# A transform and a gated feed-forward layer in one kernel: the loads and the written-out order of its first 20 microseconds

## The chip, the cores and the metric

The kernel runs on one core of a Trainium2 chip. A core has TensorE (PE: matrix products into PSUM), VectorE (DVE), ScalarE (ACT), GpSimd (POOL) and SyncE (SP), which here only issues transfers. The engines run side by side, each in the order of its own instruction list, and wait for one another through semaphores. PSUM has eight banks. The metric is the device time of one execution in microseconds (us): 486.74 as the median of three runs (485.81 to 487.13) before the change.

## The reference

```python
def _A_ref(x, w_r, w_i):
    X = jnp.fft.rfft2(x.astype(jnp.float32), axes=(-2, -1))
    X = X * (w_r + 1j * w_i)
    return jnp.fft.irfft2(X, s=(S, D), axes=(-2, -1)).astype(jnp.bfloat16)

def _B_ref(x, w_gate, w_up, w_down):
    return (_gelu(x @ w_gate) * (x @ w_up)) @ w_down

h  = x + _A_ref(_layernorm(x), A_w_r, A_w_i)
h2 = h + _B_ref(_layernorm(h), B_w_gate, B_w_up, B_w_down)
```

x is 2048 tokens by 576 features in bfloat16; `w_r` and `w_i` are 2048 by 289, the gate and up weights 576 by 4608, the down weight 4608 by 576. The first layer norm feeds a two-dimensional real Fourier transform, a product with a complex weight and the transform back; the second feeds a gated feed-forward layer.

## The kernel before, in words

All work is recorded by one class, `Prog`: each operation names the engine, what it reads and what it writes, and at the end the class puts in the semaphore waits that these names call for. It reorders nothing. So the order of each engine's list is the order in which the program text calls the operations, and for the first part of the kernel that order is a string, `SEQ1`, whose words are carried out one after another. A word's letter says what is done, its number for which tile, group or block, and a last letter, where there is one, on which engine (A for ScalarE, D for VectorE, P for GpSimd).

The 2048 tokens are held as 16 tiles of 128 in `XO` (tile c has the tokens 16p + c of partition p). The first part, called the front here, computes for each token the mean and the deviation, and the transform over 128 of the 2048 token positions as matrix products. The deviation is not put on the tokens but on the table of cosines and sines: `ATB` is the table as loaded (128 columns for each tile), `ATS` the same times one over the deviation (letter x, L522 on GpSimd for a whole group at once, L527 on VectorE tile by tile). The tiles form six groups: 0-1, 2-3, 4-6, 7-9, 10-12, 13-15. For each tile:

- B and b: statistics of the two halves of a tile on VectorE (L496), joined by v (L505); or, for three of the sixteen tiles, S and Q: sum and sum of squares on ScalarE (L488, L492, both read the whole tile), m on GpSimd (L499) and v (L508). Which tiles go to ScalarE is read from the string: those with a Q. They are 3, 4 and 13.
- q and c: for a group, the square root on ScalarE (L512) and the reciprocal on VectorE (L517).
- n and t: a negated copy and a copy of the last features into `XN` on GpSimd (L569, L574), read by the products.
- M: the products of a group (L553), five blocks of 2 m products each for a group of m tiles. Block n (0 to 29, five for each group) is accumulated in one PSUM bank.
- E: eviction of one block from PSUM to `U` in bfloat16 (L564) on ScalarE or VectorE. F: for blocks that have one, E evicts the first half of the columns and F the second.
- k: matmuls on zeros (L538), which nothing reads.

The bank of a block is set by its number alone, and blocks eight apart share one:

```python
def a_bank(i, k):
    return (5 * i + AORD.index(k) + ABASE) % 8
```

With `ABASE` 1 block n lies in bank (n + 1) mod 8. A block's products wait until the block eight before it has been evicted in full, halves included.

Behind the front stands the transform over the features (L642, `st_D`, tables `FT`), whose pairs of products go to two banks each, the first pair to banks 0 and 1, the next to 2 and 3; then a product with the 16-point tables `BT` (L662, `st_B`), the multiplication with the weights `WS` on VectorE (L675, `st_T`), products with the tables `VT` (L683 and L700), and the way back (L837, L854). Their evictions are at L608. `BT` and `VT` have parts for the first weight group or the tails, which are needed late (`BT1`, `VT1`). Copies of the weights to the other half of the partitions are made on GpSimd (L732) and VectorE (L730); GpSimd's may start when the last group's `ATS` is done. The rest of the kernel, from 55 us on, is the feed-forward layer (L946 and L1046), products nearly without a pause.

All loads of the front are issued by SP, through one helper at L242, in the order of the string `LORD`: a word x0-2 loads tiles 0 and 1, a word a0-4 the tables of tiles 0 to 3. Then come `FT`, the first part of `BT`, and the weight pieces.

Of the kernel before, what the change touches and what calls it, by code (L numbers as in the profile page):

```python
# [20 lines left out]
NPRE = 8  # L21
PARTS = ((0, 256), (256, 512))
GROUPS = ((0, 2), (2, 4), (4, 7), (7, 10), (10, 13), (13, 16))
SEQ1 = """B0 b0 S3 B2 Q3 n0 B1 b1 b2 n1 t0 m3P t2 v0 v1 n2 t1 q0 c0 k14 x0D q1 M0 E0A S4 m4P c1 x1D n3 E2A k104 b5 t3 b7 Q4 E1A M1 E7A B5 B6 E8A b6 B7 v2 q2 B11 E5A B8 c2 x2P E3A E9A b8 b9 B9 v3 E6A n4 B12 Q13 E4A k206 M2 b10 q3 c3 b11 S13 x3P E11A B10 t4 b12 v4 E10A B14 m13P E14A M3 q4 c4 x4P E12A E13A t5 b14 E15A b15 B15 v5 E16A E18D E17A q5 M4 E20A E19A E23A c5 x5D n5 E24A F24D F23D E21A M5 E25A E26D E22A E28D E27A E29D F25A F29D F26A F27A F28A F22A""".split()
LORD = "x0-2 x2-4 a0-4 x4-8 a4-8 x8-12 x12-16 a8-16".split()
SPLIT = tuple(int(w[1:-1]) for w in SEQ1 if w[0] == "F")
ACT_TILES = tuple(int(w[1:]) for w in SEQ1 if w[0] == "Q")
SEQF = """D2 D0 d2 D1 d0 d1 B2 D5 B0 d5 T2 D3 B1 d3 D4 T0 T1 B5 d4 D8 B3 d8 D7 T3 B4 d7 V0 D6 v0 V1 T5 d6 v1 R0 V2 r0 v2 T4 B6 D9 B8 T6 V3 d9 D11 v3 d11 B7 D10 B9 d10 V6 V4 T7 v6 v4 V5 B10 v5 R1 D12 T8 r1 d12 B11 T9 V7 D14 v7 T10 d14 D13 B12 d13 D15 T11 V9 T12 d15 v9 V8 B13 v8 R2 r2 T13 B14 T14 B15 V12 V10 v12 v10 V13 V11 T15 v13 V14 v11 v14 V15 R3 v15 r3""".split()
# [9 lines left out]
def _np_bf16(a):  # L38
    npdt = mybir.dt.np(BF16)
    return np.ascontiguousarray(np.asarray(a, dtype=np.float32).astype(npdt))  # L40
# [291 lines left out]
def _build(nc, A_x, A_w_r, A_w_i, B_w_gate, B_w_up, B_w_down, out):  # L332
    P = Prog(nc)
    T = build_tables()
    dram = {n: nc.inline_tensor(_np_bf16(T[n]), name="c_" + n.lower()) for n in T}
    PE, DVE, ACT, SP, POOL = "pe", "dve", "act", "sp", "pool"
# [52 lines left out]
    BT = sb.alloc("BT", [128, 2, 2, 128], BF16)  # L389
    VT = sb.alloc("VT", [128, 6, 2, 128], BF16)  # L390
# [12 lines left out]
    ATB = sb.alloc("ATB", [128, NT, 128], BF16)  # L403
# [32 lines left out]
    tabs = dram["ATAB"].rearrange("p (c k) -> p c k", c=NT)  # L436
# [1 line left out]
    def x_load(i, c0, c1):  # L438
        P.dma(SP, XO[:, c0:c1, 0:D], xv[:, c0:c1, :], f"x{i}", w=[("X", c) for c in range(c0, c1)])

    def atb_load(i, c0, c1):
        P.dma(SP, ATB[:, c0:c1, :], tabs[:, c0:c1, :], f"atb{i}", w=[("ATB", c) for c in range(c0, c1)])

    for i, w in enumerate(LORD):
        (x_load if w[0] == "x" else atb_load)(i, int(w[1:].split("-")[0]), int(w.split("-")[1]))
    P.dma(SP, FT[:, :, :].rearrange("p a b -> p (a b)"), dram["FTAB"][:, :], "ft", w=["FT"])
    P.dma(SP, BT[:, 0, :, :].rearrange("p b c -> p (b c)"), dram["BTAB"][:, 0:256], "bt", w=["BT"])

    def w_up(pl, hf):
        g0, g1 = ((0, 9), (9, 16))[hf]  # L450
# [5 lines left out]
    def w_down(pl, hf, sls=(0, 1, 2, 3), eng=SP, sem=""):  # L456
        g0, g1 = ((1, 9), (9, 16))[hf]
        src = (A_w_r, A_w_i)[pl].tensor
        for sl in sls:
            p0 = 64 * (sl // 2) + 32  # L460
            P.dma(eng, WS[p0 + sl % 2:p0 + 32:2, sl // 2, pl, g0:g1, :], bass.AP(src, (64 + 16 * (3 - sl) + 16 - g0) * K2, [[128 * K2, 16], [-K2, g1 - g0], [1, K2]]),
                  f"w{pl}{hf}{sem}", w=[("W", hf, pl, 2 + sl)])

    def w_zero(pl):
        for jp in range(2):
            P.dma(SP, WS[64 * jp + 32:64 * jp + 64, jp, pl, 0, :], bass.AP((A_w_r, A_w_i)[pl].tensor, (64 + 32 * jp) * K2, [[128 * K2, 16], [(-16 if jp else 48) * K2, 2], [1, K2]]),
                  f"wz{pl}", w=[("W", 2, pl, jp)])

    for pl in (1, 0):
        w_up(pl, 0)  # L470
        w_down(pl, 0)
    P.dma(SP, VT[:, 0, :, :].rearrange("p b c -> p (b c)"), dram["VTAB"][:, 0:256], "vt", w=["VT"])
    for pl in (1, 0):
        w_up(pl, 1)
        w_down(pl, 1, (0, 1, 2, 3) if pl else (0, 1))
    for pl in (1, 0):
        w_zero(pl)
    P.dma(SP, VT[:, 1, :, :].rearrange("p b c -> p (b c)"), dram["VTAB"][:, 256:512], "vt1", w=["VT1"])
    P.dma(SP, BT[:, 1, :, :].rearrange("p b c -> p (b c)"), dram["BTAB"][:, 256:512], "bt1", w=["BT1"])
    GORD = list(range(1, NG)) + [0]  # L480
    wkeys = [[("W", hf, pl, h) for pl in range(2) for h in range(6 if hf < 2 else 2)] for hf in range(3)]

# [12 lines left out]
    def ln1_half(c, h):  # L495
        P.op(DVE, lambda v: v.bn_stats(ST1[:, c, h, :], XO[:, c, 288 * h:288 * h + 288]), r=[("X", c)], w=[("ST1", c, h)])  # L496
# [59 lines left out]
    def a_ev(n, eng, late=False):  # L556
        i, k = n // 5, AORD[n % 5]
        hs = (1,) if late else (0,) if n in SPLIT else (0, 1)
        g0, g1 = 16 * hs[0], 16 * hs[-1] + 16
        c0, c1 = GROUPS[i]  # L560
        m, b, w = c1 - c0, a_bank(i, k), 128
        src = bank(b, 0, w, 0, 128 * m).rearrange("p (n g e) -> p n g e", n=m, g=32)[:, :, g0:g1, :]
        dst = U[0:w, k, g0:g1, c0:c1, :].rearrange("p g n e -> p n g e")
        fn = (lambda v: v.tensor_copy(dst, src)) if eng == DVE else (lambda a: a.activation(dst, src, ACTF.Copy))  # L564
        P.op(eng, fn, r=[("PS", b)] + ([("EV", n)] if late else []), w=[("U", i, k, h) for h in hs] + ([] if late else [("EV", n)]))
# [14 lines left out]
    ENG = {"A": ACT, "D": DVE, "P": POOL}  # L580
    RUN1 = {"k": idle_mm, "S": act_sum, "Q": act_sq, "B": lambda c: ln1_half(c, 0), "b": lambda c: ln1_half(c, 1), "v": ln1_var, "q": ln1_sqrt, "c": ln1_rs, "M": a_mm, "x": ln1_scale, "E": a_ev, "F": lambda n, eng: a_ev(n, eng, True), "n": x_neg, "t": x_tail, "m": act_mean2}
    P.op(ACT, lambda a: a.activation(SA[:, 0, 0:1], EPT[:, 0:1], ACTF.Sqrt), r=["EPT"], w=[("SA0", 0)])
    for w in SEQ1:
        a = w[1:]
        RUN1[w[0]](*((int(a[:-1]), ENG[a[-1]]) if a[-1] in ENG else (int(a),)))
# [8 lines left out]
    for t, w in enumerate(SEQF):  # L594
        k, i = w[0], w[1:].rstrip("abc")
        if k in "DBVR":
            b = min((b for b in used if b not in busy), key=lambda b: used[b])
# [4 lines left out]
        elif k in "dvr":  # L602
            b = FB[k.upper(), int(i)]
# [137 lines left out]
    c = 0  # L741
    while c < NT:
        c1 = c + 1
        while c not in ACT_TILES and c1 < NT and c1 not in ACT_TILES:
            c1 += 1
        src, f, keys = (SA[:, 0, c:c1], -1.0 / D, "SA0") if c in ACT_TILES else (MV1[:, c:c1, 0], -1.0, "MV1")
        P.op(POOL, lambda g, c=c, c1=c1, src=src, f=f: g.tensor_scalar(NM[:, c:c1], src, f, 1.0, op0=ALU.mult, op1=ALU.mult),
             r=[(keys, k) for k in range(c, c1)], w=[("NM", k) for k in range(c, c1)])
        c = c1
# [34 lines left out]
    for w in SEQF:  # L784
        i = int(w[1:].rstrip("abc"))
# [26 lines left out]
    for t, w in enumerate(SEQ):  # L812
        k, i = w[0], int(w[1:].rstrip("ADSP"))
        if k in "INu":
            b = min((b for b in range(2 * ing, 4) if b not in held), key=lambda b: last[b])
# [3 lines left out]
        elif k in "ioUEae":  # L819
            b = SLOT[{"i": "I", "o": "N", "U": "u", "E": "I", "a": "N", "e": "u"}[k], i] // 2  # L820
# [145 lines left out]
    for w in SEQ:  # L966
        a = w[1:]
# [53 lines left out]
    for j, c in enumerate(range(NPRE, NT)):  # L1021
        f = DEF0 + DSTEP * j
# [77 lines left out]
def bass_sequential_preLN__spectral_gfnet__geglu_ffn__prompt_kernel(  # L1100
    nc, A_x, A_w_r, A_w_i, B_x, B_w_gate, B_w_up, B_w_down, out
):
    _build(nc, A_x, A_w_r, A_w_i, B_w_gate, B_w_up, B_w_down, out)
# [28 lines left out]
```

## Time and profile before

| what | value |
|---|---|
| median of three runs | 486.74 us (485.81 to 487.13) |
| the profiled execution | 485.97 us |
| its span | 484.2 us |
| PE busy | 477.5 us (99%) |
| DVE, ACT, POOL busy | 183.3, 146.3, 52.2 us |
| first product of L553 | 7.08 us |
| first product of L642 | 19.91 us |

The profile records one execution. Its page gives for each engine the busy time and the share of the span; a chain view follows the work that ended last back from the end; a timeline lists the instructions of an engine in order of time, merged where they are alike, with the idle time ahead of an instruction and what released it in brackets. A line such as L553 is that line of the kernel before; in the kernel after, the lines from 486 to 582 have numbers smaller by two. DMA-issuing instructions stand under SPq or POOLq; the time from issue to landing is listed with them.

### The profile page before, as it was taken

The numbers are of one execution on the slowest core, as the hardware profiler recorded it, in microseconds if no ns is written. First come the engines' busy times: TensorE is split into PE (matmuls) and PEld (weight loads), VectorE is DVE, ScalarE is ACT, GpSimd is POOL, SyncE is SP. The second block draws the span as 40 slices with busy tenths as digits, with TensorE's granted clock in tenths as the row PEclk, the third lists the DMA queues.
The fourth block names the chain that finished last, engine by engine and source line by source line (L and its number), as shares of the span: only waits on it lengthen the run. The fifth ranks groups of instructions, "written<-read, shape, count | busy, mean of one in ns | idle before, by whom it ended". The sixth has DMA issues, their size and how long they took to land.

```text
span 484.2 us, 12895 instructions
## 1 busy us (share of the span) xinstructions
PE 477.5 (99%) x5875; PEld 304.4 (63%) x5876; DVE 183.3 (38%) x366; ACT 146.3 (30%) x295; POOL 52.2 (11%) x88
## 2 busy tenths in 40 slices
PE   8999999999999999999999999999999999999998
PEld 4877765555588744444688644444788544445884
DVE  7898755665500144333200234333101233333011
ACT  6998753434300032233100132223100133223000
POOL 6873317010120000000000000000000000000000
DMA  8865889941430001000000011000000000000000
GB/s 283 215 142 160 251 279 282 374 109 27 173 100 27 26 15 23 20 1 0 3 14 15 26 24 23 13 1 1 3 14 27 14 1 1 0 1 1 3 26 26
DMA packets 28582, 33.19 MB, mean 69 GB/s; under 512 B 12640, under 2 KB 21872, under 8 KB 28528
## 3 DMA queue, kind: packets, MB, share of 16 engines
q1 hardware_dynamic: 24864, 19.87, 14.3%
q0 software_dynamic: 3664, 12.50, 8.1%
q8 instruction: 46, 0.75, 0.7%
q14 instruction: 8, 0.07, 0.1%
HBM read 26.21 MB, written 2.36 MB: 59 GB/s over the span
## 4 chain that ended last, share of the span: by engine, by line
PE 95%; DMA 1%; DVE 1%; POOL 1%; SPq 0%; issue 0%; POOLq 0%; DVEq 0%
PE PS L946 58%; PE PS L1046 27%; PE PS L642 2%; PE PS L1058 2%; PE PS L683 2%; DMA XO<-in_A_x_dram 1%; PE PS L553 1%; PE PS L662 1%; PE PS L837 1%; PE PS L996 1%; DVE XO L860 1%; SPq L242 0%; PE PS L1013 0%; PE PS L854 0%; POOL XN L569 0%
## 5 line engine op out<-in xcount | busy, mean ns | idle before, releaser
L946 PE MATMUL PS<-HT,WG 64*128 64x512 bf16 (+1 forms) x2142 | 233.5, 373 | 0.1
L946 PEld LDWEIGHTS PS<-HT,WG 64*128 64x128 bf16 x2142 | 116.1, 94 | 104.4 <-DVE AT L955 0.2
L954 ACT ACTIVATE GL<-PS 128x512 bf16<-128x512 f32 x144 | 85.7, 596 | 281.7 <-PE PS L946 281.7
L955 DVE TENSOR_TENSOR AT<-GL,PS 128x512 bf16<-128x512 bf16 x144 | 98.8, 687 | 166.0 <-ACT GL L954 166.0
L1046 PE MATMUL PS<-WD,AT 64*128 64x288 bf16 x2160 | 133.0, 283 | 0.0
L1046 PEld LDWEIGHTS PS<-WD,AT 64*128 64x128 bf16 x2160 | 114.3, 94 | 18.7
L1033 DVE TENSOR_TENSOR OS<-PS,XO 128x288 bf16<-128x288 f32 (+2 forms) x32 | 13.2, 452 | 125.5 <-PE PS L1046 118.0
L946 PE MATMUL PS<-HT,WGX 64*128 64x512 bf16 x486 | 53.5, 376 | 0.0
L946 PEld LDWEIGHTS PS<-HT,WGX 64*128 64x128 bf16 x486 | 25.7, 94 | 26.7
L863 ACT ACTIVATE OS<-XO,NM 128x576 bf16<-128x576 bf16 x15 | 11.6, 773 | 11.4 <-DVE XO L1017 11.4
L642 PE MATMUL PS<-FT,U 64*128 64x288 bf16 x160 | 13.3, 283 | 0.0
L675 DVE TENSOR_TENSOR TP<-YS,WS 128x1024 bf16<-128x1024 bf16 x16 | 11.0, 686 | 0.4 <-PE PS L683 0.2
L564 ACT ACTIVATE U<-PS 128x384 bf16<-128x384 f32 (+2 forms) x31 | 10.5, 427 | 1.2 <-PE PS L553 1.1
L496 DVE BATCH_NORM_STATS2 ST<-XO 128x6 f32<-128x288 bf16 x26 | 10.0, 441 | 1.8 <-DMA XO<-in_A_x_dram 1.8
L242 POOL DMA_DIRECT2D WG<-in_B_w_gate_dram x9 | 6.1, 679 | 35.5 <-DMA WG<-in_B_w_gate_dram 32.1
L683 PE MATMUL PS<-VT,TP 64*128 64x128 bf16 x256 | 9.9, 217 | 0.0
L553 PE MATMUL PS<-ATS,XO 128*128 128x128 bf16 x96 | 8.2, 220 | 1.5 <-POOL ATS L522 0.8
L242 POOL DMA_DIRECT2D WD<-in_B_w_down_dram x9 | 6.7, 756 | 22.9 <-PE PS L1013 22.9
L608 ACT ACTIVATE CUS<-PS 128x576 bf16<-128x576 f32 x14 | 9.1, 656 | 0.4 <-PE PS L642 0.2
L1058 PE MATMUL PS<-WD,AT 128*128 128x448 bf16 (+1 forms) x72 | 9.0, 286 | 0.0
L538 PE MATMUL PS<-ZD 128*128 128x512 bf16 x23 | 7.5, 484 | 1.5 <-POOL ZD L431 1.5
L608 ACT ACTIVATE YS<-PS 128x576 bf16<-128x576 f32 x14 | 8.8, 653 | 0.1
(88 smaller groups left out, 231.3 us busy)
## 6 DMA issues: line engine op xcount, KB each, us to landing
WD<-in_B_w_down_dram POOLq DMA_DIRECT2D x9, 576.0 KB, 13.0
WG<-in_B_w_up_dram SPq DMA_DIRECT2D x6, 576.0 KB, 6.6
WG<-in_B_w_gate_dram POOLq DMA_DIRECT2D x6, 576.0 KB, 6.2
out_dram<-OS SPq DMA_DIRECT2D x30, 72.0 KB, 1.7
XO<-in_A_x_dram SPq DMA_DIRECT2D x3, 576.0 KB, 7.1
WGX<-in_B_w_up_dram SPq DMA_DIRECT2D x2, 576.0 KB, 4.5
WGX<-in_B_w_gate_dram POOLq DMA_DIRECT2D x2, 576.0 KB, 5.8
HT<-HN SPq DMA_TRANSPOSE x60, 2.4
```

The costliest lines, as they stand in the source:

```text
L242: fn = lambda e: e.dma_start(out_ap, in_ap)
L553: P.op(PE, lambda t, b=b, lhs=lhs, p0=p0, p1=p1, s=s, e=e, o=o, c=c: t.matmul(bank(b, p0, p1, o, o + 128), lhs, ATS[:, c, :], start=s, sto ...
L608: fn = (lambda v: v.tensor_copy(dst, src)) if eng == DVE else (lambda a: a.activation(dst, src, ACTF.Copy))
L642: return P.op(PE, lambda t: t.matmul(bank(b0 + o, 0, 128, 0, 2 * HK), U[64 * h:64 * h + 64, us, 2 * i:2 * i + 2, :, :], FT[64 * h:64 * h + ...
L683: return P.op(PE, lambda t: t.matmul(bank(b0 + o, 0, 128, 128 * c, 128 * c + 128), TP[64 * h:64 * h + 64, z, o, t_, c:256:2], VT[64 * h:64 ...
L863: P.op(ACT, lambda a, c=c, out=out: a.activation(out, XO[:, c, 0:D], ACTF.Square, bias=NM[:, c:c + 1], accum_out=SB2[:, 1, c:c + 1]), r=[( ...
L946: op = P.op(PE, lambda t, h0=h0, kt=kt, wt=wt, b=b, s=(not second and j == 0), e=(second and j == n - 1): t.matmul(bank(b, 0, 128, c0, c1) ...
L954: P.op(ACT, lambda a: a.activation(GL[:, s2, :], bank(b0), ACTF.Gelu_apprx_tanh), r=[("PS", b0)], w=[("GL", s2)])
L955: P.op(DVE, lambda v: v.tensor_tensor(AT[:, f, :], GL[:, s2, :], bank(b0 + 1), op=ALU.mult), r=[("GL", s2), ("PS", b0 + 1)], w=[("AT", f)])
L1033: P.op(DVE, lambda v: v.tensor_tensor(OS[:, p % 2, d0:d1], bank(b, 0, 128, 0, d1 - d0), XO[:, c, d0:d1], op=ALU.add), r=[("PS", b), ("X", ...
L1046: e[h] = P.op(PE, lambda t, f=f, h=h, r0=r0, j=j: t.matmul(bank(b0 + h, 0, 128, 0, 288), AT[r0:r0 + 64, f, 128 * p:128 * p + 128], WD[r0:r ...
L1058: P.op(PE, lambda t, b=b, d0=d0, d1=d1, f=f, j=j: t.matmul(bank(b, 0, 128, 0, d1 - d0), AT[:, f, 128 * p:128 * p + 128], WD[:, f, d0:d1], ...
```

## The change

Four things are changed together.

- `LORD`: the tiles are loaded in two-tile pieces (0-1, 2-3, 4-5, 6-7, 8-9, 10-11) and one piece of four (12-15) one after another; the tables of tiles 8 to 15 follow as before.
- The tables of tiles 0 to 3 and 4 to 7 are issued by ScalarE, behind its dummy square root; the second waits until tiles 0 and 1 have landed.
- `BT` is loaded whole in one transfer, and `VT`'s first two parts in one, at the places of the first transfers of each; the two later transfers are gone from SP's list.
- `SEQ1` is a new order of the front. The tiles on ScalarE are 3, 5 and 9. The scale of groups 0 and 1 is on GpSimd (x0P, x1P) in place of VectorE. The idle matmuls k104 and k206 are gone, k14 stays. The blocks evicted in halves are 25, 27, 28 and 29, all halves on ScalarE; VectorE evicts blocks 18, 23 and 24 whole.

```diff
-SEQ1 = """B0 b0 S3 B2 Q3 n0 B1 b1 b2 n1 t0 m3P t2 v0 v1 n2 t1 q0 c0 k14 x0D q1 M0 E0A S4 m4P c1 x1D n3 E2A k104 b5 t3 b7 Q4 E1A M1 E7A B5 B6 E8A b6 B7 v2 q2 B11 E5A B8 c2 x2P E3A E9A b8 b9 B9 v3 E6A n4 B12 Q13 E4A k206 M2 b10 q3 c3 b11 S13 x3P E11A B10 t4 b12 v4 E10A B14 m13P E14A M3 q4 c4 x4P E12A E13A t5 b14 E15A b15 B15 v5 E16A E18D E17A q5 M4 E20A E19A E23A c5 x5D n5 E24A F24D F23D E21A M5 E25A E26D E22A E28D E27A E29D F25A F29D F26A F27A F28A F22A""".split()
-LORD = "x0-2 x2-4 a0-4 x4-8 a4-8 x8-12 x12-16 a8-16".split()
+SEQ1 = """b1 t0 B1 b0 S3 n0 n1 B0 m3P t1 B2 v0 Q3 b2 v1 q0 q1 c0 S5 Q5 x0P k14 M0 b4 c1 B4 E1A B7 x1P m5P t2 B6 b6 v2 n2 b8 S9 b7 m9P q2 c2 B10 B8 Q9 v3 E0A b11 x2P E3A E4A M1 E2A q3 b10 E5A B11 E6A c3 M2 E9A t3 E11A b12 B12 E7A n3 v4 E8A q4 E13A x3P n4 b15 B14 E10A M3 c4 E14A B15 E12A b14 E15A B13 x4P E16A b13 v5 t4 q5 n5 E19A E18D M4 c5 E17A x5D E21A t5 E20A E23D E22A M5 E26A E27A E24D E25A E28A E29A F27A F28A F25A F29A""".split()
+LORD = "x0-2 x2-4 x4-6 x6-8 x8-10 x10-12 x12-16 a8-16".split()
-    def atb_load(i, c0, c1):
-        P.dma(SP, ATB[:, c0:c1, :], tabs[:, c0:c1, :], f"atb{i}", w=[("ATB", c) for c in range(c0, c1)])
+    def atb_load(i, c0, c1, eng=SP, r=()):
+        P.dma(eng, ATB[:, c0:c1, :], tabs[:, c0:c1, :], f"atb{i}", r=r, w=[("ATB", c) for c in range(c0, c1)])
-    P.dma(SP, BT[:, 0, :, :].rearrange("p b c -> p (b c)"), dram["BTAB"][:, 0:256], "bt", w=["BT"])
+    P.dma(SP, BT[:, :, :, :].rearrange("p a b c -> p (a b c)"), dram["BTAB"][:, :], "bt", w=["BT", "BT1"])
-    P.dma(SP, VT[:, 0, :, :].rearrange("p b c -> p (b c)"), dram["VTAB"][:, 0:256], "vt", w=["VT"])
+    P.dma(SP, VT[:, 0:2, :, :].rearrange("p a b c -> p (a b c)"), dram["VTAB"][:, 0:512], "vt", w=["VT", "VT1"])
-    P.dma(SP, VT[:, 1, :, :].rearrange("p b c -> p (b c)"), dram["VTAB"][:, 256:512], "vt1", w=["VT1"])
-    P.dma(SP, BT[:, 1, :, :].rearrange("p b c -> p (b c)"), dram["BTAB"][:, 256:512], "bt1", w=["BT1"])
     P.op(ACT, lambda a: a.activation(SA[:, 0, 0:1], EPT[:, 0:1], ACTF.Sqrt), r=["EPT"], w=[("SA0", 0)])
+    atb_load(8, 0, 4, ACT)
+    atb_load(9, 4, 8, ACT, [("X", 0)])
```

## The prediction

> **What bounds the kernel now.** I read the page first: TensorE (PE) is busy almost throughout, and the chain that ended last is PE work too. So a change to the front shows in the total as the time by which the first stage behind it, the products of L642, starts earlier or later; behind that PE runs on in its order, and nothing of it is edited.
>
> ```profile
> PE 477.5 (99%) x5875; PEld 304.4 (63%) x5876; DVE 183.3 (38%) x366; ACT 146.3 (30%) x295; POOL 52.2 (11%) x88
> PE 95%; DMA 1%; DVE 1%; POOL 1%; SPq 0%; issue 0%; POOLq 0%; DVEq 0%
> ```
>
> Next the chain over the first 75 us. It waits for the token tiles 8 to 11 until 10.14, then for GpSimd, and from 14.53 on it is PE alone: two stretches of L553, then L642.
>
> ```profile
> 3.06 7.08 DMA XO<-in_A_x_dram
> 11.65 0.83 POOL ATS L522
> 13.64 0.84 POOL ATS L522
> 14.53 1.85 PE PS L553 x30
> 16.47 3.51 PE PS L553 x60
> 19.98 2.01 PE PS L642 x30
> ```
>
> Then the timelines of three queues: SP's issues (start, length), PE, and ScalarE (ACT). From 11.78 to 20.84 ACT has no idle note: it is as full as PE in the front, and it empties the PSUM banks that PE fills.
>
> ```profile
> 1.64 0.43 SPq L242 DMA_DIRECT2D ATB<-c_atab  x1
> 2.11 0.43 SPq L242 DMA_DIRECT2D XO<-in_A_x_dram  x1
> 3.06 0.91 SPq L242 DMA_DIRECT2D XO<-in_A_x_dram  x2
> ...
> 10.46 1.24 PE L538 MATMUL PS<-ZD 128*128 128x512 bf16 x5
> 12.54 0.23 PE L553 MATMUL PS<-ATS,XO 128*128 128x128 bf16 x1 [0.84 <-POOL ATS L522]
> 19.91 2.08 PE L642 MATMUL PS<-FT,U 64*128 64x288 bf16 x30
> ...
> 7.85 0.68 ACT L488 ACTIVATE JNK<-XO 128x576 bf16<-128x576 bf16 x1
> 8.51 0.37 ACT L564 ACTIVATE U<-PS 128x256 bf16<-128x256 f32 x1
> 15.00 2.00 ACT L564 ACTIVATE U<-PS 128x384 bf16<-128x384 f32 x5
> 16.85 0.34 ACT L512 ACTIVATE RS<-MV,EPT 128x3 f32<-128x3 f32 x1
> 17.03 3.81 ACT L564 ACTIVATE U<-PS 128x384 bf16<-128x384 f32 x13
> 21.05 1.26 ACT L608 ACTIVATE CUS<-PS 128x576 bf16<-128x576 f32 x2 [0.20 <-PE PS L642]
> ```
>
> Last the transfers' issues with their time to landing, taken stretch by stretch (size, us to landing):
>
> ```profile
> ATB<-c_atab SPq DMA_DIRECT2D x1, 128.0 KB, 4.0
> XO<-in_A_x_dram SPq DMA_DIRECT2D x1, 576.0 KB, 5.5
> ATB<-c_atab SPq DMA_DIRECT2D x1, 128.0 KB, 5.8
> XO<-in_A_x_dram SPq DMA_DIRECT2D x1, 576.0 KB, 7.1
> ATB<-c_atab SPq DMA_DIRECT2D x1, 256.0 KB, 8.4
> ```
>
> Issue plus time gives the landings: tiles 0-1 at 3.6, 2-3 at 4.5, tables 0-3 at 5.6, tiles 4-7 at 7.6, tables 4-7 at 8.4, tiles 8-11 at 10.1, 12-15 at 11.5, tables 8-15 at 12.4.
>
> **The change, part by part.** *Loads.* SP still issues eight transfers before the one for FT, so each later slot stays (0.43 us each). In place of two table loads among the tiles there are four two-tile pieces, and both small table loads go to ACT. The time that matters, called t8, is the landing of tiles 8-9. Counted in KB landed, 1440 of tiles and 256 of tables stand ahead of its end: 1696, half way between 1408 (8.4) and 1984 (10.1), so 9.26. Bounds: 6.95, if each of three pieces takes the 0.82 us that lay between tiles 0-1 and 2-3 and the tables cost nothing; 10.1, if each takes the 1.2 us of the slowest step (tables 0-3) and the tables keep their 1.2 and 0.8. I take 9.26, since the bytes are the same and only their order is new.
> The Trainium skill ("DMA: Bandwidth & Descriptors", section "Issuing engines are not separate DMA queues") says that transfers started by different engines run on the same 16 DMA engines and interleave, so that a second issuer saves only issue time. By it the tables still stand ahead, and 9.26 holds; without it the table bytes drop out, 1440 KB are left, and t8 is 8.5, a sum 0.8 us lower. No row of before has a load on ACT's queue.
>
> *ACT's issues.* Two of about 0.43 us (SP's row), at 2.2 behind the table load and the dummy square root, and at 3.7 behind tiles 0-1. ACT idled 2.18 us there until 4.40, so they cost nothing; if tiles 2-3 landed before 4.15, they would cost the difference. The first table load is issued 0.6 later than now; 4.0 us on it lands at 6.2. GpSimd then has just ended L574 for tiles 2-3 (0.30+0.62+0.62+0.26+0.30 with gaps of 0.1, from 3.75), and the first scale, moved from VectorE's two of 0.21 to one on GpSimd of about 0.6 (0.83 for 384 columns), starts at 6.6 behind the reciprocal. So the first L553 starts at 7.3, not 7.08. That 0.2 is covered by what follows.
>
> *ACT's queue.* The new list puts the sum and square of tile 9 (S9, Q9) behind one eviction of the first group (E1A) and ahead of all its others. E1A is issued at about 7.95 and ACT is free at 8.2; then S9 stands and waits for tiles 8-9, with E0A, E3A, E4A and E2A queued behind it. Block n goes to bank (n+1) mod 8, so block 8 (the fourth of M1) waits for E0A and M2's first block (10) for E2A. Steps from the rows: S or Q 0.66 (7.85 to 8.51), square root 0.18 between evictions, an eviction of 256 columns 0.275, of 384 0.37 (five in 1.85), of 192 0.255. E0A starts at t8 + 0.66 + 0.18 + 0.66 + 0.06 = t8+1.56 and E2A ends at t8+2.77: 12.0. M2 began at 12.54 before, so here 0.5 is won. GpSimd's scale of that group is done at 11.5 (S9's sum, 0.3, 0.9) and lies beside the wait.
>
> *The end of ACT's queue.* From S9 on ACT holds: S9 and Q9 1.32, four square roots 0.72, nine evictions of 256 columns 2.46, thirteen of 384 4.81, and six halves up to F25A with its own end 1.90: 11.2, with 0.1 for two short waits 11.3. F25A frees bank 2, and the second L642 set (D0) writes banks 2 and 3. So D0 starts at t8 + 11.3 = 20.56. Before it started at 20.16 (19.91 plus four of L642 at 0.061, ten taking 0.61). The loss is 0.4 us; break-even is t8 = 8.86, and from there each microsecond of t8 costs one. PE itself would be ready sooner: M3 at 13.8, M4 15.7, M5 17.4 to 19.1, against 19.8; what it wins is lost in front of D0, because the four second halves, of which VectorE had some before, are all on ACT now.
>
> *Fillers.* Ten idle matmuls (L538, 1.03 and 1.24 us) go. They stood in waits, so nothing is won. PE is then idle from 9.1 to 11.2 in M1, where the longest idle before, once PE ran fast, was 0.84. I take its cost at nothing; the other end is the first rival.
>
> *Tables of the 16-point stage.* BT and VT as one transfer each: 64 KB more in front of the w loads (about 0.2 us at 288 KB in 0.82), two issues (0.58, 0.43) gone from SP at 25 to 26. BT was needed first at 21.8 and landed at 14.4, VT at 26.6 and landed at 20.1; the w copies on VectorE start at 20.8 and have slack until 22.9. SP's next wait is at 29.2. Nothing; were the w loads 1 us late, up to the whole of it.
>
> Sum: +0.4. The profiled execution took 485.97 (span 484.2 and 1.8 around it), so 486.4; the runs' median lies 0.77 above it, so 487.1, with 0.1 for the extra bytes 487.2.
>
> **The rivals.**
> *PE goes slow in the gap (slower).* At the start L538 needs 0.427 us a matmul for 4.2 us, then 0.216: there is a slow state, and the fillers may have held it off. If the idle 2.1 us bring it back, some 39 of M2's and M3's products take 0.11 (twice the warm 0.056, as 0.427 is of 0.216) instead: 2.0 us, M5 ends at 21.1, F25A at about 21.8, D0 1.6 to 1.8 later than before: 488.5. It decides once the slow stretch passes 1.5 us, PE's slack ahead of D0. For it: the fillers are gone where the gap is longest. Against: 0.84 idle in 12.54's neighbourhood left the products at 0.056.
> The Trainium skill ("TensorE: Matmul & The Clock Gate", section "Why this matters for your kernels") advises against PE-idle gaps over about 3 us between bursts, since a whole idle window brings the half rate back. By that rule 2.1 us would not, and the sum stays; a gap grown by 1 us would. No row of before tests it.
> *The table loads on ACT land late (slower).* S9 cannot start before the landing of tables 0-3 + 1.7 (scale, the first block, E1A). At 6.2 that is hidden; at 2.25 + 5.8 (row of tables 4-7) = 8.05 it replaces t8 by 9.75: 487.6; beyond 8.6 it is over 488.2. The 8.4 row is the far end.
> *The pieces land early.* At t8 of 8.2 or less E1A bounds S9: D0 at 19.5, 0.6 won, 486.1. For it: from 9 to 12 us the windows show 405 to 418 GB/s, at which three pieces take 2.1 us. It is a floor, since the rest of ACT's queue is unchanged.
> *The change does more behind the front* (SP freer from 25 us): nothing waits there; 485.2 or less, if at all.
>
> **How the numbers follow.** Forecast 0.44 (487.2, own range 486.4 to 488.3 with t8 from 8.5 to 10.1), slow PE 0.24, late tables 0.14, early pieces 0.13, gain behind 0.05. 0.3% is 1.46 us, about what a measurement of this kernel can tell from no change (three runs lie within 1.3). Slower by that: 0.24x0.8 + 0.14x0.6 + 0.44x0.12 = 0.33. Faster: 0.05 and a tenth of the early case, 0.06. Same: 0.61. The range runs from the early case, less 0.2 of spread, to slow PE with 0.3: 485.9 to 488.8.
>
> **What would show it.** Right: ACT idle before L488 of tile 9 on a tile transfer until about 9.3; PE idle about 2 us in the second L553 set with an ACT eviction as releaser; L642 with a gap of near 1 us after its first products; products at 0.056 throughout. Wrong: products at 0.11 after 11; the first scale waiting for ATB; ACT idle at the end of the front; S9 starting at 8.2.

## The result and the profile after

The kernel after takes 487.62 us (median of ten executions, 487.21 to 488.95), the kernel before 486.46 beside it (ten, 485.81 to 487.35). The ratio is 1.0029, with a 95% interval of 1.0020 to 1.0038: a small loss, real, and about as large as a measurement of this kernel can tell. The forecast was 487.2 in a range of 485.9 to 488.8; it started from 486.74, the median of three, so the change that was forecast is +0.46, and the one measured is +1.16. The profiled execution of after took 487.71 us (span 485.9), that of before 485.97 (span 484.2), so the two traces lie 1.7 us apart where the medians lie 1.16 apart; the one of before happens to be a quick one.

The page of after, busy time by engine and then the shares of the chain that ended last, is still TensorE's:

```profile
PE 476.3 (98%) x5866; PEld 279.5 (58%) x5866; DVE 183.8 (38%) x358; ACT 146.3 (30%) x295; POOL 54.1 (11%) x91
PE 93%; DVE 2%; ACT 2%; DMA 1%; POOL 1%; issue 0%; SPq 0%; DVEq 0%
```

PE is busy 1.2 us less than before and the kernel is longer all the same, so PE waits more. TensorE's timeline in after shows where (start, length, operation; in brackets the idle time ahead and its releaser):

```profile
8.06 0.23 PE L551 MATMUL PS<-ATS,XO 128*128 128x128 bf16 x1 [1.09 <-POOL ATS L520]
...
10.94 0.40 PE L551 MATMUL PS<-ATS,XO 128*128 128x128 bf16 x4 [0.93 <-ACT U L562]
12.19 0.22 PE L551 MATMUL PS<-ATS,XO 128*128 128x128 bf16 x1 [0.63 <-ACT U L562]
...
14.55 0.22 PE L551 MATMUL PS<-ATS,XO 128*128 128x128 bf16 x1 [0.52 <-POOL ATS L520]
...
20.09 0.47 PE L642 MATMUL PS<-FT,U 64*128 64x288 bf16 x4
21.16 1.77 PE L642 MATMUL PS<-FT,U 64*128 64x288 bf16 x26 [0.60 <-ACT U L562]
```

The first product comes at 8.06 (before 7.08). By 14.55, the fourth group, both kernels are level (before 14.53). The first set of L642 starts at 20.09 (before 19.91), but only four of its thirty products run; the other 26 stand until 21.16, where they ran at 20.16 before. So 1.0 us is lost in front of the second set, 0.60 of it as PE's idle time with an eviction of ScalarE as its releaser.

ScalarE's timeline in after, its DMA issues (ACTq) included:

```profile
0.73 1.28 ACT L580 ACT_TABLE_LOAD   x1 [0.73 <-PEq L1117]
0.86 0.33 ACTq L242 DMA_DIRECT2D ATB<-c_atab  x1
2.03 0.20 ACT L580 ACTIVATE SA<-EPT 128x1 f32<-128x1 f32 x1
4.43 0.33 ACTq L242 DMA_DIRECT2D ATB<-c_atab  x1
5.35 0.68 ACT L486 ACTIVATE JNK<-XO 128x576 bf16<-128x576 bf16 x1 [3.12 <-DMA XO<-in_A_x_dram]
...
9.01 0.67 ACT L486 ACTIVATE JNK<-XO 128x576 bf16<-128x576 bf16 x1
...
13.06 1.04 ACT L562 ACTIVATE U<-PS 128x384 bf16<-128x384 f32 x3 [0.35 <-PE PS L551]
...
19.06 2.27 ACT L562 ACTIVATE U<-PS 128x384 bf16<-128x384 f32 x9 [0.41 <-PE PS L551]
```

Three things are to be seen. The first table load was issued at 0.86, while the engine was still loading its activation table: it stands behind the dummy square root in the program, but nothing makes it wait for it. The sum of tile 9 at 9.01 has no idle note, so tiles 8-9 were there already. And the last nine evictions run in one row from 19.06; the eighth of them, the second half of block 25, ends at 21.1 and frees the bank for which PE stands.

The transfers in after (size, us from issue to landing) at 0.73 and 0.86, at 2.59 (tiles 8-9), and at 4.43:

```profile
XO<-in_A_x_dram SPq DMA_DIRECT2D x1, 288.0 KB, 3.7
ATB<-c_atab ACTq DMA_DIRECT2D x1, 128.0 KB, 3.7
...
XO<-in_A_x_dram SPq DMA_DIRECT2D x1, 288.0 KB, 5.4
...
ATB<-c_atab ACTq DMA_DIRECT2D x1, 128.0 KB, 6.2
```

Issue plus time, each transfer by itself, gives the landings:

| what | before | after |
|---|---|---|
| tiles 0-1 | 3.7 | 4.4 |
| tiles 2-3 | 4.4 | 5.3 |
| tables 0-3 | 5.7 | 4.6 |
| tiles 4-5, 6-7 | 7.7 | 6.5, 7.2 |
| tiles 8-9, 10-11 | 10.1 | 8.0, 8.7 |
| tables 4-7 | 8.4 | 10.6 |
| tiles 12-15 | 11.5 | 10.5 |
| tables 8-15, the last of 2816 KB | 12.4 | 11.1 |

So the first four tiles come 0.7 to 0.9 us later and all later tiles 0.4 to 2.2 us earlier; tables 4-7 come 2.2 later. (The 3.6 and 4.5 of the prediction for the first two pieces are 3.7 and 4.4 when each issue is read by itself, so the step between them is 0.7 and not 0.82. Only its lower bound for tiles 8-9 rests on that.)

Behind the front, the first product of L837 starts at 44.77 against 43.62 (+1.15), and then the products wait longer for `VR`. TensorE's timeline in after, and below it the same place before:

```profile
44.77 1.16 PE L837 MATMUL PS<-DT,V 64*128 64x288 bf16 x16 [0.38 <-DVE V L608]
46.70 0.35 PE L837 MATMUL PS<-DT,VR 64*128 64x288 bf16 x2 [0.77 <-DMA VR<-RB]
...
57.20 1.05 PE L946 MATMUL PS<-HT,WG 64*128 64x256 bf16 x16
```

```profile
43.62 1.16 PE L837 MATMUL PS<-DT,V 64*128 64x288 bf16 x16 [0.38 <-DVE V L608]
45.10 0.34 PE L837 MATMUL PS<-DT,VR 64*128 64x288 bf16 x2 [0.33 <-issue]
```

From the first product of L837 to the first with `VR` it is 1.93 us after and 1.48 before, so 0.45 more. The first product of L946 starts at 57.20 (before 55.47): 1.7 us, all of the difference of the two traces.

### The profile page after: what moved, and what is told of

It is laid out like the page before. It is cut to its first block, busy times and chain, and to the rows that moved or that the text cites. A ratio compares the mean times of both kernels' runs of the same rounds, so it can differ in the third digit from the quotient of the medians.

```text
span 485.9 us, 12874 instructions
## 1 busy us (share of the span) xinstructions
PE 476.3 (98%) x5866; PEld 279.5 (58%) x5866; DVE 183.8 (38%) x358; ACT 146.3 (30%) x295; POOL 54.1 (11%) x91
## 4 chain that ended last, share of the span: by engine, by line
PE 93%; DVE 2%; ACT 2%; DMA 1%; POOL 1%; issue 0%; SPq 0%; DVEq 0%
PE PS L946 58%; PE PS L1046 27%; PE PS L1058 2%; PE PS L642 1%; DVE ST L494 1%; PE PS L551 1%; DMA XO<-in_A_x_dram 1%; PE PS L683 1%; DMA VR<-RB 1%; PE PS L996 1%; DVE XO L860 1%; PE PS L662 1%; ACT YS L608 1%; ACT CUS L608 0%; PE PS L837 0%
## 5 line engine op out<-in xcount | busy, mean ns | idle before, releaser
L946 PE MATMUL PS<-HT,WG 64*128 64x512 bf16 (+1 forms) x2142 | 233.3, 372 | 0.1
L946 PEld LDWEIGHTS PS<-HT,WG 64*128 64x128 bf16 x2142 | 105.9, 94 | 114.4 <-DVE AT L955 0.2
L1046 PEld LDWEIGHTS PS<-WD,AT 64*128 64x128 bf16 x2160 | 103.3, 94 | 29.8
L946 PE MATMUL PS<-HT,WGX 64*128 64x512 bf16 x486 | 53.4, 376 | 0.0
L946 PEld LDWEIGHTS PS<-HT,WGX 64*128 64x128 bf16 x486 | 23.2, 94 | 29.2
L863 ACT ACTIVATE OS<-XO,NM 128x576 bf16<-128x576 bf16 x15 | 11.6, 774 | 11.4 <-DVE XO L1017 11.4
L642 PE MATMUL PS<-FT,U 64*128 64x288 bf16 x160 | 13.5, 283 | 0.7 <-ACT U L562 0.6
L494 DVE BATCH_NORM_STATS2 ST<-XO 128x6 f32<-128x288 bf16 x26 | 10.1, 440 | 2.5 <-DMA XO<-in_A_x_dram 2.5
L562 ACT ACTIVATE U<-PS 128x384 bf16<-128x384 f32 (+2 forms) x31 | 10.3, 437 | 0.8 <-PE PS L551 0.8
L551 PEld LDWEIGHTS PS<-ATS,XO 128*128 128x128 bf16 x96 | 6.8, 98 | 4.4 <-ACT U L562 2.1
```

The costliest lines, as they stand in the source:

```text
L551: P.op(PE, lambda t, b=b, lhs=lhs, p0=p0, p1=p1, s=s, e=e, o=o, c=c: t.matmul(bank(b, p0, p1, o, o + 128), lhs, ATS[:, c, :], start=s, sto ...
L642: return P.op(PE, lambda t: t.matmul(bank(b0 + o, 0, 128, 0, 2 * HK), U[64 * h:64 * h + 64, us, 2 * i:2 * i + 2, :, :], FT[64 * h:64 * h + ...
L946: op = P.op(PE, lambda t, h0=h0, kt=kt, wt=wt, b=b, s=(not second and j == 0), e=(second and j == n - 1): t.matmul(bank(b, 0, 128, c0, c1) ...
L1046: e[h] = P.op(PE, lambda t, f=f, h=h, r0=r0, j=j: t.matmul(bank(b0 + h, 0, 128, 0, 288), AT[r0:r0 + 64, f, 128 * p:128 * p + 128], WD[r0:r ...
```

## The experiments

Two causes were to be told apart. **T, the tail:** the last evictions, with all second halves on ScalarE, hold the bank of the second set of L642. **L, the loads:** the table load that ScalarE issues at 0.86 runs beside the first tiles and delays everything that starts from them. Each kernel is the changed one with one edit, unless its diff says otherwise; the lines of L642 and L837 have numbers lower by one or two where load lines are taken out. The times of before beside them are 486.38 (35 executions) for four of the kernels (the tail alone, the first table in SP's list, the old loads, the old order) and 486.56 (29) for the other four. Each ratio and its interval come from the executions and are not exactly the quotient of the two medians.

**The tail alone.** The words behind block 23 are put in such an order that VectorE evicts block 24 ahead of M5, and behind M5 block 26, the first half of 28 and both halves of 29; on ScalarE the second half of 25 comes ahead of those of 27 and 28.

```diff
-... E20A E23D E22A M5 E26A E27A E24D E25A E28A E29A F27A F28A F25A F29A
+... E20A E23D E24D E22A M5 E25A E26D E27A E28D F25A E29D F27A F28A F29D
```

> The changed kernel with another order of the last evictions alone: blocks 26, 28 and both halves of 29 on VectorE, F25A in front of F27A and F28A on ScalarE; loads as changed. Theory T (tail): nine evictions in a row on ScalarE behind the second block of M5 (19.06 to 21.1) hold bank 2, and the second set of L642 starts at 21.16; with four of them on VectorE it starts at about 20.4, the first set stays at 20.1, and the time falls by 0.7, to 486.9. Theory L (loads): the loss comes from tiles 0 to 3 landing 0.8 us late; then the tail matters by 0.2 at most, 487.4.

Measured 486.43 us, ratio to before 0.9999 (0.9983 to 1.0015). The timelines of this kernel, ScalarE's, VectorE's and TensorE's:

```profile
19.32 1.06 ACT L562 ACTIVATE U<-PS 128x192 bf16<-128x192 f32 x4 [0.34 <-PE PS L551]
...
18.04 2.69 DVE L562 CAST U<-PS 128x384 bf16<-128x384 f32 x6
...
7.97 0.23 PE L551 MATMUL PS<-ATS,XO 128*128 128x128 bf16 x1 [1.84 <-POOL ATS L520]
...
19.88 2.07 PE L642 MATMUL PS<-FT,U 64*128 64x288 bf16 x30
```

Four evictions stand in ScalarE's last row where nine did, and VectorE does six from 18.04 on. The thirty products of L642 run in one piece from 19.88; four at 0.061 into it, the second set starts at 20.12, 1.04 earlier than in the changed kernel. That is 0.3 more than the 20.4 expected. The first product of the front is as late as there (7.97). T is shown, and the loss is gone with this edit alone. Which part of it does so, the sharing or the earlier second half of block 25, is not told apart.

**The first table in SP's list.** Tables 0 to 3 return to SP's third place, the second table load stays on ScalarE.

```diff
-LORD = "x0-2 x2-4 x4-6 x6-8 ...
+LORD = "x0-2 x2-4 a0-4 x4-6 x6-8 ...
-    atb_load(8, 0, 4, ACT)
```

> The changed kernel with the tables of tiles 0 to 3 back in SP's third slot; those of tiles 4 to 7 stay on ScalarE. Theory L: tiles 0-1 land at 3.7 again and not at 4.4, statistics, GpSimd's queue and the first L551 move 0.7 forward, L642 starts at about 19.4, its second set at 20.4, and the time falls by 0.7, to 486.9. Theory T: what is won at the start is lost in front of the tail, the second set of L642 stays near 21, 487.4. If the landing of tiles 0-1 stays at 4.4, it was not the table load on ScalarE that delayed it.

Measured 486.75 us, ratio 1.0004 (0.9988 to 1.0020). Its timelines, VectorE's first statistics and TensorE's L642 (here L641):

```profile
3.74 1.90 DVE L494 BATCH_NORM_STATS2 ST<-XO 128x6 f32<-128x288 bf16 x5 [1.82 <-DMA XO<-in_A_x_dram]
...
20.58 1.76 PE L641 MATMUL PS<-FT,U 64*128 64x288 bf16 x26 [0.60 <-ACT U L562]
```

The statistics start at 3.74 where after has 4.43, and the second set comes 0.58 earlier; the idle 0.60 with ScalarE as its releaser is untouched. So L is shown as well, as a cause of its own: the delay of 0.7 at the first tile is 0.6 at the end of the front, and T stands behind it unchanged. It is the trace that shows it; the interval of the time reaches up to 1.0020, where that of the changed kernel begins.

**Both edits together.**

> The changed kernel with both repairs: the tables of tiles 0 to 3 in SP's third slot, and the last evictions shared with VectorE. Theory: the two losses lie one behind the other (0.6 at the first tiles, 1.1 at the second set of L642), so both gains add: L642 starts at about 19.3 without a gap, 0.6 earlier than before, 485.8 against 486.4. Rival: VectorE or GpSimd bound the front by then, and the second gain is lost: 486.4.

Measured 486.09 us, ratio 0.9990 (0.9981 to 1.0000). TensorE's timeline:

```profile
19.32 2.07 PE L641 MATMUL PS<-FT,U 64*128 64x288 bf16 x30
...
43.67 1.16 PE L836 MATMUL PS<-DT,V 64*128 64x288 bf16 x16 [0.34 <-DVE V L607]
```

The second set is at 19.32 + 0.24 = 19.56: 1.60 earlier than in the changed kernel, against 1.04 + 0.58 from the two edits alone. In the front they add up. The front now ends 0.6 earlier than before the change, but L837 starts at 43.67, where it started at 43.62: in this profile the gain has gone on the way through the stages between. The time is the lowest of all that were run, 0.5 below before where 0.6 was expected, and its interval reaches to no change.

**All loads in SP's list.** As the last, and the second table load too returns to SP, behind tiles 6-7.

```diff
-LORD = "x0-2 x2-4 a0-4 x4-6 x6-8 x8-10 ...
+LORD = "x0-2 x2-4 a0-4 x4-6 x6-8 a4-8 x8-10 ...
-    atb_load(9, 4, 8, ACT, [("X", 0)])
```

> The kernel with both repairs, and the tables of tiles 4 to 7 in SP's list too, behind tiles 6-7: nothing is issued by ScalarE. They land at about 8.3 in place of 10.5; tiles 8-9 land 0.4 to 0.8 later, at 8.4 to 8.8, where the sum of tile 9 starts at 8.4 anyhow. GpSimd's scale of the third group stands behind that sum. If the issue by ScalarE buys nothing: the same as with both repairs, within 0.3. If it buys 0.4 or more: slower by as much.

Measured 486.47 us, ratio 1.0000 (0.9986 to 1.0015). The transfers issued at 3.07, and TensorE's timeline:

```profile
ATB<-c_atab SPq DMA_DIRECT2D x1, 128.0 KB, 4.8
```

```profile
19.25 2.07 PE L640 MATMUL PS<-FT,U 64*128 64x288 bf16 x30
...
45.88 0.35 PE L835 MATMUL PS<-DT,VR 64*128 64x288 bf16 x2 [1.57 <-DMA VR<-RB]
```

Tables 4 to 7 land at 7.9 instead of 10.3 in the last kernel, and that moves L642 by 0.07: nothing was waiting for them there. All 2816 KB have landed at 4.97 + 6.5 = 11.4, against 12.4 before, on the same single queue: the smaller pieces alone account for most of the earlier landings. The front is as short as in the last kernel and L837 starts at 43.16, but the wait for `VR` is 1.57 in this profile, which eats that.

**The old loads under the new order.** `LORD` as before the change, nothing issued by ScalarE, the new `SEQ1`.

```diff
-LORD = "x0-2 x2-4 x4-6 x6-8 x8-10 x10-12 x12-16 a8-16".split()
+LORD = "x0-2 x2-4 a0-4 x4-8 a4-8 x8-12 x12-16 a8-16".split()
-    atb_load(8, 0, 4, ACT)
-    atb_load(9, 4, 8, ACT, [("X", 0)])
```

> The new order (and the joined 16-point tables) with the loads of before. The prediction's formula: tile 9 lands with tiles 8 to 11 at 10.14, ScalarE waits for it until then, the second set of L642 starts at 10.14 + 11.3 = 21.4, 1.3 later than before: 487.8. Theory L alone: tiles 0-1 at 3.7 give back 0.7, so 486.9. Theory T: the tail costs 0.8 in any case, 487.3 or more.

Measured 488.40 us, ratio 1.0033 (1.0017 to 1.0050). ScalarE's and TensorE's timelines:

```profile
8.00 0.68 ACT L486 ACTIVATE JNK<-XO 128x576 bf16<-128x576 bf16 x1 [1.16 <-DMA XO<-in_A_x_dram]
...
10.46 0.68 ACT L486 ACTIVATE JNK<-XO 128x576 bf16<-128x576 bf16 x1 [0.76 <-DMA XO<-in_A_x_dram]
...
14.76 1.04 ACT L562 ACTIVATE U<-PS 128x384 bf16<-128x384 f32 x3 [0.58 <-PE PS L551]
...
12.41 0.61 PE L551 MATMUL PS<-ATS,XO 128*128 128x128 bf16 x4 [2.29 <-ACT U L562]
...
22.34 1.77 PE L640 MATMUL PS<-FT,U 64*128 64x288 bf16 x26 [0.60 <-ACT U L562]
```

Here ScalarE does stand in front of the sums of tile 5 (1.16) and tile 9 (0.76), as the prediction had it for tile 9 in the changed kernel, and the second set comes 1.2 later still, 0.9 later than the 21.4 expected. Of that 0.9, 0.3 is the tile's (10.46 for 10.14). The other 0.6 is ScalarE's wait ahead of 14.76 for products that ran at half rate: here the prediction's first rival came. PE had stood idle for 2.29, and its products from 12.41 to 15.15 follow each other 0.107 apart and not 0.056 (four of them take 0.61 in the row above, 0.40 at the same place in after); the granted clock is 0.50 in these three microseconds.

So the new order needs the smaller pieces: with them it takes its sums without a wait and PE's idle time stays short; with the old ones it loses on both.

**The new loads under the old order.** `SEQ1` as before the change, the rest as after.

> The changed loads with the order of before. Theory L: first statistics at 4.4, the first L553 at about 7.9 (7.08 before), VectorE reaches the third group 0.5 late and stays late: 486.9, between the two kernels. Theory T or a fault of the new order in general: 486.4, as before, or less, since tiles 8 to 11 land 1.5 to 2 us earlier than before.

Measured 487.15 us, ratio 1.0021 (1.0004 to 1.0037). TensorE's timeline:

```profile
8.44 0.23 PE L551 MATMUL PS<-ATS,XO 128*128 128x128 bf16 x1 [2.37 <-DVE ATS L525]
...
21.10 2.08 PE L642 MATMUL PS<-FT,U 64*128 64x288 bf16 x30
```

The old order has no gap in L642, but all of it is 1.2 late, from the first product on (8.44, before 7.08). The profiled execution took 488.18, 1.0 above the median of the eleven, so this 1.2 is not to be set against the 0.8 of the medians. The late first tiles cost this order its whole front, and the earlier later tiles bring it nothing: GpSimd waits 0.79, 0.40 and 0.24 for VectorE's reciprocals, so it is VectorE, which starts on the first tile, that is late.

**The 16-point tables alone.** The kernel before with `BT` and `VT` in one transfer each and nothing else changed.

> The kernel before with the joined 16-point tables alone. Prediction and both theories: nothing, 486.4; the last products with VR (L837) wait 0.3 as before. If the joined tables are what makes those products wait longer in the changed kernel (0.77), the wait grows here too and the time rises by 0.4.

Measured 486.73 us, ratio 1.0001 (0.9991 to 1.0010): no effect on the time. TensorE's timeline:

```profile
20.12 2.08 PE L640 MATMUL PS<-FT,U 64*128 64x288 bf16 x30
...
46.01 0.34 PE L835 MATMUL PS<-DT,VR 64*128 64x288 bf16 x2 [0.69 <-DMA VR<-RB]
```

This profile has the order of before and reaches L642 0.2 later, and the products with `VR` 0.9 later. That is what one profile may differ by from another behind the front; readings there of less than a microsecond prove little.

**Both table loads held back.** In the changed kernel the first table load on ScalarE waits for tiles 0-1 and the second for tiles 2-3.

```diff
-    atb_load(8, 0, 4, ACT)
-    atb_load(9, 4, 8, ACT, [("X", 0)])
+    atb_load(8, 0, 4, ACT, [("X", 0)])
+    atb_load(9, 4, 8, ACT, [("X", 2)])
```

> The changed kernel with both table loads on ScalarE held until tiles have landed: the first until tile 0, the second until tile 2. If the early issue alone delays tiles 0 and 1, they land at 3.7. If a load on ScalarE's queue is served slowly behind SP's long list (6.0 to 6.8 us for the second table so far, against 3.7 for the first into an empty queue), the first tables land at about 9.8, the first L551 starts at 10.5 and the time rises to 489 or more. If the queue alone costs nothing, they land at 7.5, the first L551 starts at 8.2, as changed, and the time stays at 487.6.

Measured 490.71 us (two executions), ratio 1.0086 (1.0062 to 1.0110). GpSimd's timeline, and below it the transfers issued between 3.6 and 3.8:

```profile
10.34 1.37 POOL L520 TENSOR_TENSOR ATS<-ATB,RS 128x256 bf16<-128x256 bf16 x2 [4.00 <-DMA ATB<-c_atab]
```

```profile
XO<-in_A_x_dram SPq DMA_DIRECT2D x1, 576.0 KB, 6.5
ATB<-c_atab ACTq DMA_DIRECT2D x1, 128.0 KB, 6.6
```

Issued at 3.68, the 128 KB are there at 10.3, and GpSimd stands four microseconds for them. The first product comes at 11.01, 2.95 later than in the changed kernel, the second set of L642 3.0 later, and the time is 3.1 above the changed kernel's. PE had stood idle for 3.68 by then, and its first 26 products came 0.107 apart here too; that hardly shows at the second set, since GpSimd's list, 3.0 late, sets the pace behind it. At that moment SP's seven tile loads are all issued, and the small load on the other queue lands together with the 576 KB that SP issued beside it: a second queue gives no right of way. In SP's third place (tables 0 to 3, 1.65), with the small pieces behind it, the same 128 KB took 3.0 to 3.1. So the early issue at 0.86, which costs 0.7 to 0.9 at the first tiles, is still far better than a later one on this queue; the cheap place is in SP's list. This bears out the rule of the Trainium skill ("DMA: Bandwidth & Descriptors", section "Issuing engines are not separate DMA queues") by which transfers of all issuers share the engines and a second issuer saves issue time only.

## Why the prediction was right, and where it was wrong

The direction, the place (the second set of L642, held by an eviction of ScalarE) and the size class were right. The size was low: +0.4 at the second set and +0.5 in all were forecast, +1.0 and +1.16 came. Inside, two of its steps failed, in opposite directions, and a third thing, how full GpSimd's list is, was not seen. Of the four signs that it named, two came (the gap in L642 and products at 0.056 throughout); ScalarE's wait for tile 9 did not, and the two microseconds of idle PE came in pieces.

- **Loads: wrong.** t8 was to be 9.26, "since the bytes are the same and only their order is new". It was 8.0. Smaller pieces land sooner for the same bytes: 1280 KB were there at 7.2 (before 7.7), 2816 KB at 11.1 (12.4), and at 11.4 in one queue. And only one table stood ahead of tiles 8-9, since the one issued at 4.43 landed at 10.6. The estimate without the table bytes, 8.5, was too late as well.
- **ScalarE's issues: wrong.** They were put at 2.2 and 3.7, at no cost. The first went out at 0.86, inside the engine's table load, which ran until 2.01: an issue with nothing to wait for did not stand behind it. It landed at 4.6 and not 6.2, so the first scale never waited for it; but tiles 0-3 landed 0.7 to 0.9 late, and the first product came at 8.06 instead of 7.3. That the price is 0.6 to 0.7 in the front was shown by putting the load back.
- **ScalarE's queue: the number right, the reason wrong.** The sum of tile 9 was to start at 9.26 behind a wait for the tile. It started at 9.01 with no wait, as the rival of early pieces had it; that rival's 486.1 failed because the eviction ahead of the sum came at 8.74, not 7.95, on account of the late first tiles, and because 12.15 and not 11.3 followed the sum. Two errors of 1.3 and 0.8 thus nearly cancelled: that the sum's start came out 0.25 from the forecast is luck. M2's first block started at 12.19 for a forecast of 12.0, and that is luck too (next point). The wait itself is real where the tiles come late: 0.76 with the old loads.
- **The end of ScalarE's queue: right in kind, too small.** From the sum of tile 9 to the second set 11.3 was counted, with 0.1 in it for waits; it took 21.16 - 9.01 = 12.15. Of the missing 0.85, 0.66 is the two waits for PE, 0.35 and 0.41, less the 0.1 that was counted. Behind both stands GpSimd, and this is the term that was not counted: with two more scales on it GpSimd's list is full.

  The first wait, ahead of 13.06, is for M2's second block. M2 began at 12.19. The row names ScalarE as the releaser, but the eviction that M2's first block needs had ended at 11.7, and the scale of M2's tiles ends on GpSimd at 11.22 + 0.83 = 12.05. In all six kernels with the new order and the small pieces M2 begins 0.14 to 0.15 after that scale, whatever ScalarE does. The kernel with all loads in SP's list shows it: ScalarE's row ends at 11.38, the scale at 11.33, and PE starts at 11.48, 0.15 behind the scale and only 0.10 behind the eviction, where in after these are 0.14 and 0.5.

```profile
10.20 1.18 ACT L562 ACTIVATE U<-PS 128x256 bf16<-128x256 f32 x4
...
10.50 0.83 POOL L520 TENSOR_TENSOR ATS<-ATB,RS 128x384 bf16<-128x384 bf16 x1 [0.17 <-POOL TM L497]
...
11.48 0.22 PE L551 MATMUL PS<-ATS,XO 128*128 128x128 bf16 x1 [0.24 <-ACT U L562]
```

  The prediction had that scale done at 11.5, beside the wait. The second wait, ahead of 19.06, is for M5, whose products were to be ready at 17.4 and ran at 18.19, right behind M4. M3 and M4 ran at 14.55 and 16.51 for 13.8 and 15.7, again 0.14 to 0.15 after the ends of GpSimd's scales (14.40 and 16.37). GpSimd's timeline in after:

```profile
7.39 1.37 POOL L520 TENSOR_TENSOR ATS<-ATB,RS 128x256 bf16<-128x256 bf16 x2 [0.31 <-DVE RS L515]
...
11.22 0.83 POOL L520 TENSOR_TENSOR ATS<-ATB,RS 128x384 bf16<-128x384 bf16 x1 [0.17 <-POOL TM L497]
...
13.57 0.83 POOL L520 TENSOR_TENSOR ATS<-ATB,RS 128x384 bf16<-128x384 bf16 x1 [0.17 <-DVE MV L503]
14.56 0.83 POOL L567 TENSOR_SCALAR XN<-XO 128x768 bf16<-128x768 bf16 x1 [0.16 <-POOL ATS L520]
15.54 0.83 POOL L520 TENSOR_TENSOR ATS<-ATB,RS 128x384 bf16<-128x384 bf16 x1
```

From 7.39 to 18.15 it has no idle stretch over 0.2. (The 0.17 ahead of 13.57 is GpSimd's usual gap, though the row names VectorE: the reciprocal that the scale needs had been ready since 12.53.) The scale of the fourth group starts at 13.57, as before (13.64), although two of its three tiles, 8 and 9, landed 2.2 earlier. With the first table back in SP's list GpSimd's first scale starts at 6.69 and M3 at 13.96: the list moves with its start, by 0.70 and 0.59, less a longer wait there for tables 4-7. So PE could not be sooner than before at M3 while the first tiles were late, and the tail's delay stood on top. This is read from the timelines; no run takes a scale off GpSimd.

- **"What it wins is lost in front of D0, because the four second halves ... are all on ACT now": right** in place and engine: with the last evictions reordered and shared the gap is gone and so is the loss. That it is the halves alone is not shown.
- **Fillers: right in this kernel, in part by luck.** PE stood for 0.93 and 0.63 with eight products between (some 2 in one piece were forecast), and for 1.09 ahead of the first product, and all products that follow start 0.056 apart. The rival of a slow PE (488.5) did not come, but only because the idle time came in pieces: with the old loads PE stood for 2.29 in one piece, about what was forecast here, and 26 products followed 0.107 apart, as that rival had it (there it cost 0.6 at the second set, where the rival's 1.6 to 1.8 lie 1.2 to 1.4 above the forecast's 0.4). Idle time of 3.68 (both loads held back) did the same, and 2.37 ahead of the first product of the old order did not. What decides between 2.29 and 2.37 is not shown. The rule of the Trainium skill ("TensorE: Matmul & The Clock Gate", section "Why this matters for your kernels"), by which PE should have no idle gaps over some 3 us, would have let the 2.29 pass; the measurement differs, and it decides.
- **`BT` and `VT`: right**, shown alone (1.0001).
- **Late tables (487.6): did not come** in the changed kernel; the kernel with the loads held back shows the mechanism at its far end.
- **Behind the front: 0.45 that no step had**, the longer wait for `VR`. The last transfer of `VR` is issued by GpSimd, as in before, in a group of five that starts 3.5 us ahead of L837, as before; it landed 5.07 us after the first of the five (41.28 to 46.35; it is issued at 43.22 and takes 3.1), before after 4.4 (40.07 to 44.4; issued at 42.02, it took 2.4). The idle time at that place was 0.77 here and 0.43, 0.72, 0.69, 0.40, 1.57 and 0.78 in six of the experiments, in none of them in step with the edit; in the other two no such wait was in the way. The joined tables alone do not bring it, since those other two have them as well. What sets it is open. The median's 1.16 leaves room for little more than the 1.0 of the front, so part of the 0.45 may belong to that one profile.

## What to carry to other kernels

A load moved to another engine's queue goes out when that engine's sequencer reaches it, not when the engine is free (0.86 here, in a table load that ran until 2.01), and it competes with what others issued (tiles 0-1 took 3.7 and not 2.9): where it should land is decided by what is issued ahead of it, so keep a small urgent load in its place in one list. When evictions are dealt out at the end of a stage, count for each PSUM bank that the next stage needs which eviction frees it and how many stand ahead of that one on its engine. A queue that is moved onto (here GpSimd's) is to be added up in full, not only at the step that moves. When idle matmuls are taken out, look at the longest idle time that is left in one piece: 2.29 us brought the half rate here.

## What the runs showed of the hardware that was not expected

- A DMA issue on ScalarE's sequencer started at 0.86, 0.13 into an activation table load of 1.28.
- 128 KB issued on ScalarE's queue took 3.6 to 3.8 us beside the first tile load (and that one 3.6 to 3.7 instead of 2.9 to 3.0), and 5.9 to 7.0 behind seven or eight loads of SP; in SP's list, with the small pieces, 3.0 to 3.1 in the third place and 4.8 in the sixth.
- Tile loads of 288 KB in place of 576, with the same bytes in one queue, brought the last of 2816 KB in at 11.4 us instead of 12.4 (12.8 and 13.0 in the other two kernels with the old loads).
- After PE had been idle for 2.29 us (old loads) and for 3.68 us (both table loads held back) the granted clock was 0.50 for about 3.4 us, and the products were 0.107 apart instead of 0.056. After 2.37 us (old order) they were 0.056 apart.
- In GpSimd's full list an instruction that waits for the one before it on the same engine starts some 0.16 us after it (0.16 with `ATS` of L520 as releaser, above). Between 5.6 and 14.6 there are eight gaps of 0.15 to 0.18, five of them of this kind: 1.3 us of a list that sets the pace.
